# Light convolution and feed-forward: the second product in nine slots a pair, with two banks that swap halves, and the work around it placed anew

## The chip, the cores and the metric

The kernel runs on one core of a Trainium2 chip. The metric is device time of one execution in microseconds (us). The five engines of the core that matter here are TensorE (PE, with its weight loads as PEld), VectorE (DVE), ScalarE (ACT), GpSimd (POOL) and SyncE (SP, which only issues DMAs).

## What is computed

The reference is a depthwise causal convolution of 7 taps (weights by head, through a softmax), then a feed-forward layer with a clipped square between its two products, all in float32:

```python
# x: (8, 4096, 192), weight: (8, 7) -> tokens: 32768 rows of 192
out = np.einsum('hk,bskhg->bshg', softmax(weight), x_unf)   # x_unf: the last 7 rows of each row
# feed-forward, d_ff = 2048
h = x @ w_in
g = np.where(h >= 1, h, np.where(h <= -1, 0.0, (h + 1) ** 2 / 4))
return g @ w_out
```

## The kernel before

**Tiles.** The 32768 tokens are cut into 64 blocks of 512 tokens (`s`). The 2048 hidden channels are cut into 8 pairs (`j`) of two 128-channel chunks (`e`). A step `q` is one pair of one block: 512 steps. Two blocks make a group of 16 steps (`i` = 0 to 15), for which the convolution is worked in three units: "a" (128 channels of the first block), "b" (128 channels of the second) and "r" (the remaining 64 channels of both).

**Precision.** Blocks 0 and 1 (the first 16 steps) use plain float32 matmuls, which cost more passes. The other 62 blocks (496 steps) use float32r operands, each number split in a high part (`hi`, `gh`, first half of `W`) and a low part (`lo`, `gl`), so that a product is high x high + low x high + high x low.

**Two matmuls at a time.** Every matmul contracts 64 rows: one in the upper half of the array's rows (partitions 0 to 63, `TOP`) and its partner in the lower half (`BOT`). The two run side by side and write different PSUM banks. I call such a pair of matmuls a slot.

**A step.** `mm1(q)` makes h for pair q: 18 matmuls, 9 slots, into one of two h buffers of two banks each. `mm2(q - 2)` (`DELAY = 2`) adds the second product of an earlier pair into four accumulator banks: `m0`, `m1` for 128 output channels (one bank for each half of the array), `r0`, `r1` for the other 64 (beside their own low-part product, since 64 channels leave room). That is 20 matmuls, 10 slots: high x high on m in four matmuls a half (the weight's two parts), gl on m in two, gh and gl on r in two each.

**Between the products**, for the later blocks: VectorE clips h to -1..1 (L463), ScalarE squares (L469), VectorE takes the maximum with h (L474); a step later ScalarE casts to the high part (L481) and VectorE subtracts to get the low part (L487). `g`, `gh` and `gl` have three buffers each.

**Accumulators.** After pair 7 of a block, `evac` copies the four banks out on ScalarE (L498, L499), GpSimd adds m0 + m1 and r0 + r1 (L501), ScalarE moves the lower half of r up (L511), GpSimd adds it (L512), VectorE transposes (L524), and SyncE's queue stores.

**The order of the work.** Each engine runs its own instructions in the order in which the code writes them; semaphores do the rest. Tables (`PLAN_A`, `PLAN_B`, `PLAN_R`) say in which of the 16 steps which tap of which unit is done, and when a unit is transposed ("T") or split into high and low parts. A tap is a product on ScalarE (L219, L226 for the first) and an addition on GpSimd (L230). `Chunk.hi` and `Chunk.lo` prepare the weights' parts during the first 16 steps.

## Time and profile before

| | |
|---|---|
| median of three runs | 2256.98 us (2256.78 to 2256.98) |
| the profiled execution: span from first to last instruction | 2255.6 us |
| TensorE busy | 2249.6 us, 100% of the span |
| VectorE busy | 2103.2 us, 93% |
| ScalarE busy | 1697.6 us, 75% |
| GpSimd busy | 1168.4 us, 52% |
| granted TensorE clock | 1.000 |

How to read the profile's rows. A row of a group has the source line, the engine, the operation, its output and inputs by the program's tile names, the shapes and the count; then busy time in us and the mean of one in ns; then the idle time of the engine just before such instructions, and who ended it. A row of a timeline has the start in us, the duration, and the same names; idle time before it stands in brackets with its releaser. A row of a line's own view has the least, median and greatest duration in ns. A row on DMAs has the size and the median time in us from issue to landing. Names ending in q are queues. A matmul's end is modelled, its start is measured.

### The profile page before, as it was taken

The numbers are of one execution on the slowest core, as the hardware profiler recorded it, in microseconds if no ns is written. First come the engines' busy times: TensorE is split into PE (matmuls) and PEld (weight loads), VectorE is DVE, ScalarE is ACT, GpSimd is POOL, SyncE is SP. The second block draws the span as 40 slices with busy tenths as digits, with TensorE's granted clock in tenths as the row PEclk, the third lists the DMA queues.
The fourth block names the chain that finished last, engine by engine and source line by source line (L and its number), as shares of the span: only waits on it lengthen the run. The fifth ranks groups of instructions, "written<-read, shape, count | busy, mean of one in ns | idle before, by whom it ended". The sixth has DMA issues, their size and how long they took to land.

```text
span 2255.6 us, 48202 instructions
## 1 busy us (share of the span) xinstructions
PE 2249.6 (100%) x19645; PEld 1842.2 (82%) x19645; DVE 2103.2 (93%) x1883; ACT 1697.6 (75%) x2153; POOL 1168.4 (52%) x868
## 2 busy tenths in 40 slices
PE   9999999999999999999999999999999999999999
PEld 6988888888888888888888888888888888888887
DVE  8899999999999999999999999999999999999997
ACT  7677877778777787777877777877778777787775
POOL 1446644556445565454654455644556545565441
PEclk9999999999999999999999999999999999999999
DMA  7222222222222212222222222222222222212211
GB/s 158 49 51 48 42 46 47 51 53 39 51 49 46 53 34 51 49 49 51 41 46 47 49 51 51 39 49 46 49 53 39 51 49 46 54 35 50 49 34 24
DMA packets 442125, 110.84 MB, mean 49 GB/s; under 512 B 410288, under 2 KB 417840, under 8 KB 441904
## 3 DMA queue, kind: packets, MB, share of 16 engines
q1 hardware_dynamic: 441744, 107.66, 25.8%
q8 instruction: 155, 2.54, 0.5%
q14 instruction: 66, 0.54, 0.1%
q10 hardware_dynamic: 160, 0.10, 0.0%
HBM read 32.84 MB, written 25.17 MB: 26 GB/s over the span
## 4 chain that ended last, share of the span: by engine, by line
PE 100%; ACT 0%; DVE 0%; issue 0%; DVEq 0%; POOL 0%; POOLq 0%; ACTq 0%
PE h L408 47%; PE accm L452 30%; PE accr L452 20%; PE accr L426 1%; PE accm L426 1%; PE accr L190 0%; PE accm L602 0%; PE accr L408 0%; PE accm L181 0%; PE h L155 0%; PE h L553 0%; PE accr L646 0%; ACT xT L168 0%; ACT xT L165 0%; ACT xT L167 0%
## 5 line engine op out<-in xcount | busy, mean ns | idle before, releaser
L230 POOL TENSOR_TENSOR y<-y,p 128x512 f32<-128x512 f32 x546 | 765.5, 1402 | 730.8 <-DVE g L474 559.5
L487 DVE TENSOR_TENSOR gl<-g,gh 128x1024 fp32r<-128x1024 f32 (+1 forms) x497 | 732.1, 1473 | 27.6 <-ACT gh L481 23.6
L469 ACT ACTIVATE g<-g 128x1024 f32<-128x1024 f32 (+1 forms) x505 | 535.3, 1060 | 242.4 <-DVE g L463 232.9
L463 DVE TENSOR_SCALAR g<-h 128x1024 f32<-128x1024 f32 (+1 forms) x505 | 609.8, 1208 | 97.1 <-PE h L408 88.1
L481 ACT CAST gh<-g 128x1024 fp32r<-128x1024 f32 (+1 forms) x497 | 521.7, 1050 | 237.1 <-DVE g L474 225.6
L408 PE MATMUL h<-hi,w 64*128 64x512 f32 x4032 | 629.8, 389 | 0.0
L474 DVE TENSOR_TENSOR g<-h,g 128x1024 f32<-128x1024 f32 (+1 forms) x505 | 613.4, 1215 | 12.1 <-ACT g L469 4.5
L452 PE MATMUL accm<-gh,w 64*128 64x512 f32 x3966 | 535.0, 388 | 0.0
L408 PEld LDWEIGHTS h<-hi,w 64*128 64x128 f32 x4032 | 382.6, 184 | 81.9
L452 PEld LDWEIGHTS accm<-gh,w 64*128 64x128 f32 x3966 | 372.3, 184 | 81.8 <-issue 0.2
L408 PE MATMUL h<-lo,w 64*128 64x512 f32 x2016 | 399.6, 388 | 0.0
L219 ACT ACTIVATE p<-xT,wk 128x512 f32<-128x512 f32 x562 | 375.1, 710 | 0.0
L452 PE MATMUL accm<-gl,w 64*128 64x512 f32 x1984 | 308.1, 388 | 0.0
L452 PE MATMUL accr<-gl,wr 64*128 64x512 f32 x1984 | 308.0, 388 | 0.0
L452 PE MATMUL accr<-gh,wr 64*128 64x512 f32 x1984 | 308.0, 388 | 0.0
L408 PE MATMUL h<-rh,w 64*128 64x512 f32 x992 | 306.0, 388 | 0.0
L408 PE MATMUL h<-rhi,w 64*128 64x512 f32 x992 | 306.0, 388 | 0.0
L408 PEld LDWEIGHTS h<-lo,w 64*128 64x128 f32 x2016 | 193.3, 184 | 41.5 <-DMA lo<-lo 0.3
L501 POOL TENSOR_TENSOR sum<-t 128x512 f32<-128x512 f32 (+1 forms) x124 | 160.7, 1316 | 126.3 <-ACT t L499 126.3
L452 PEld LDWEIGHTS accm<-gl,w 64*128 64x128 f32 x1984 | 186.4, 184 | 40.9
L452 PEld LDWEIGHTS accr<-gh,wr 64*128 64x128 f32 x1984 | 186.4, 184 | 40.9
L452 PEld LDWEIGHTS accr<-gl,wr 64*128 64x128 f32 x1984 | 186.4, 184 | 40.9
(145 smaller groups left out, 1976.8 us busy)
## 6 DMA issues: line engine op xcount, KB each, us to landing
out_dram<-osb SPq DMA_DIRECT2D x366, 64.0 KB, 2.0
raw<-in_x_dram SPq DMA_DIRECT2D x334, 68.0 KB, 2.4
hi<-hi SPq DMA_DIRECT2D x126, 128.0 KB, 2.3
lo<-lo SPq DMA_DIRECT2D x126, 128.0 KB, 2.3
rhi<-rh SPq DMA_DIRECT2D x62, 128.0 KB, 2.2
rlo<-rl SPq DMA_DIRECT2D x62, 128.0 KB, 2.3
words<-in_moe_w_in_dram SPq DMA_DIRECT2D x16, 192.0 KB, 4.0
words<-in_moe_w_out_dram SPq DMA_DIRECT2D x8, 384.0 KB, 5.0
```

Source lines behind the costliest of these rows:

```text
L219: nc.scalar.mul(p, self.xT[:, SH + k:SH + k + TB], wk[:, self.wsel, k:k + 1])
L230: nc.gpsimd.tensor_add(y, y, self.product(k))
L408: nc.tensor.matmul(h[e], w[HALVES[e], c0:c0 + P], x[e][e], start=(n == 0), stop=(n == len(mms) - 1))
L426: nc.tensor.matmul(accs[s][a, i][:, c0:c0 + D], g[half, e, b * P:(b + 1) * P], w[half, e, :], start=(j == 0 and e == 0 and b % 2 == 0), st ...
L452: nc.tensor.matmul(accs[s][a, i], st, g[HALVES[i], e, :], start=(j == 0 and n == first[a]), stop=(j == NPAIR - 1 and n == last[a]))
L463: nc.vector.tensor_scalar(out=g[:, e, :], in0=hs[q][:, e, :], scalar1=-1.0, scalar2=1.0, op0=ALU.max, op1=ALU.min)
L469: nc.scalar.activation(g[:, e, :], g[:, e, :], AF.Square, bias=0.5, scale=0.5)
L474: nc.vector.tensor_tensor(out=g[:, e, :], in0=h[:, e, :], in1=g[:, e, :], op=ALU.max)
L481: nc.scalar.copy(gh[:, e, :], gs[q][:, e, :])
L487: eng.tensor_sub(gl[:, e, :], g[:, e, :], gh[:, e, :])
L501: nc.gpsimd.tensor_add(y[:, n], t[0][:, n], t[1][:, n])
```

## The change

Seven things change together. `LATE = 3` comes into force after the first two blocks, so `mm2` runs three pairs behind `mm1`.

1. **Nine slots.** w_out's 192 columns are cut into X, Y, Z of 64. The two 128-column weight tiles of a half are arranged so that a pair needs three turns of three slots. In each turn a half has one kind of columns: X and Y, X and Z, or Z and Y, where a stationary tile holds high parts for the one and low parts for the other. The first two slots of a turn are the pair's two chunks with `gh`, the third is with a low part of g: `gl0` or `gl1` for one chunk, or their sum `gt` (a new VectorE addition, L528), with its own weight tile `WL` whose columns come in part by DMA from the high parts of both chunks.
2. **Two banks swap halves.** In the first turn the upper half writes r0 and the lower half r1, in the second m0 and m1, in the third r1 and r0. In odd pairs the turns run the other way round, so that neighbouring pairs begin and end with the same banks. Before the third turn (L474) TensorE waits for a semaphore, `turns`, raised after the second turn's first slot (L481). The source writes this as `drain(fusable=True).then_inc`; in the built program the matmul before it carries the increment and no instruction for the drain is left.
3. **Relu for clip.** ScalarE does relu (L507) and square (L508); VectorE does minimum and maximum in one instruction (L513, `most`). VectorE's clip goes.
4. **Order in a step.** ScalarE: relu and square of q, the accumulators' copies if a block is done, taps, then the cast of q - 1 (before: the cast came first). VectorE: the low part of q - 2 and its sum, transposes and taps, then the maximum of q.
5. **Accumulators.** ScalarE copies the four banks in the order m0, m1, r1, r0 (L552), in step j = 2. The sums are four accumulating DMAs, issued on GpSimd's queue in steps j = 3 and j = 4 (L561); the second two read what the first two wrote. Transposes and stores follow in steps 6 and 7 (before: 2 and 3).
6. **Taps of A on VectorE** (`taps_dve`, L215) from the second group on, and new tables that spread the taps; loads of "a" and "r" are issued two steps earlier.
7. **The weights' parts** are made by other subtractions (L389 to L394) and four small DMAs a chunk; the last block's sum (`evac_last`) is written anew; pools are listed in another order, and the one matmul of 128 rows (`WHOLE`) goes.

The core of the diff:

```diff
+LATE = 3
...
+        def lo(self, rest):
...
+            nc.vector.tensor_sub(w[:, :, 2, x], f[:, :, z], w32[:, :, 1, y])
+            nc.vector.tensor_sub(v[:, 1, x], f[:, 1, x], w32[:, 0, 0, x])
+            nc.vector.tensor_sub(v[:, 2, y], f[:, 0, y], w32[:, 1, 0, y])
+            for to, src in ((v32[:, 0, x], w32[:, 0, 0, x]), (v32[:, 0, y], w32[:, 1, 0, y]),
+                            (v32[:, 1, y], w32[:, 1, 1, y]), (v32[:, 2, x], w32[:, 0, 1, y])):
+                nc.sync.dma_start(out=to, in_=src)
...
+    XY, XZ, ZY = range(3)
+    BANKS = (("r", 0), ("m", 0), ("r", 1)), (("r", 1), ("m", 1), ("r", 0))
+    PARTS_OF = (XZ, XY, ZY), (ZY, XY, XZ)
+    turns = tc.alloc_semaphore("turns")
+    turn = [0]
+
+    def leave(mm):
+        nc.tensor.drain(fusable=True).then_inc(turns, 1)
+        turn[0] += 1
+
+    def enter():
+        nc.tensor.wait_ge(turns, turn[0])
+
     def mm2(q):
...
-        m0, m1, r0, r1, r = ("m", 0, gh), ("m", 1, gh), ("m", 0, gl), ("r", 0, gh), ("r", 0, gl)
-        mms = [(e, m) for ms in ((m0, m1), (r0,), (r1,), (r,)) for e in range(2) for m in ms]
...
+        low = {XY: gt, XZ: gl[:, 1, :], ZY: gl[:, 0, :]}
+        seen = set()
+        for k in range(9):
+            for i, half in enumerate(HALVES):
+                turned = k // 3 if j % 2 == 0 else 2 - k // 3
+                bank, part = BANKS[i][turned], PARTS_OF[i][turned]
+                w, g = ((wg[:, k % 3, part], gh[:, k % 3, :]) if k % 3 < 2
+                        else (wl[:, part], low[part]))
+                if i == 0 and k == 6:
+                    enter()
+                mm = nc.tensor.matmul(accs[s][bank], w[half], g[half],
...
+                if i == 1 and k == 3:
+                    leave(mm)
...
+    def act_both(q):
+        g = gs[q] = act.tile([P, 2, TB], F32, name="g", bufs=3)
+        for e in tiles(q):
+            nc.scalar.activation(g[:, e, :], hs[q][:, e, :], AF.Relu, bias=0.5, scale=0.5)
+            nc.scalar.activation(g[:, e, :], g[:, e, :], AF.Square)
...
+        nc.vector.tensor_add(gt, gl[:, 0, :], gl[:, 1, :])
...
+    def evac_banks(s):
+        acc = accs.pop(s)
+        t = {}
+        for bank in (("m", 0), ("m", 1), ("r", 1), ("r", 0)):
+            t[bank] = ob.tile([P, TB], F32, name="t", bufs=4)
+            nc.scalar.copy(t[bank], acc[bank])
...
+    def evac_add(s, step):
+        t = sums[s] if step == 0 else sums.pop(s)
+        m, r = t["m", 0], t["r", 0]
+        for to, src in (((m, t["m", 1]), (r[BOT], t["r", 1][TOP])) if step == 0 else
+                        ((m[TOP], r[TOP]), (m[BOT], t["r", 1][BOT]))):
+            nc.gpsimd.dma_start(out=to, in_=src, accum_op=ALU.add)
...
-    PLAN_A = {4: ("T", 0), 5: (1, 2), 6: (3, 4), 7: (5, 6), 8: "split"}
+    PLAN_A = {1: ("T",), 2: (0, 1), 3: (2,), 4: (3,), 8: (4,), 9: (5,), 10: (6,), 11: "split"}
...
+            if q < NQ:
+                act_both(q)
+            if done is not None and done % NPAIR == NPAIR - 1:
+                (evac if done < NF32 else evac_banks if done < NQ - 1 else evac_last)(
+                    done // NPAIR)
...
+            if q - 2 in ghs and q - 2 not in gls:
+                act_lo(q - 2)
+            if q < NQ:
+                if s > 2 and j in (3, 4):
+                    evac_add(s - 1, j - 3)
+                m = 6 if s > 2 else 2
+                if m <= j < m + 2:
+                    store(s - 1, "mr"[j - m])
+                conv_slot(i, conv_b, conv_n.get("a"), conv_n.get("r"))
+            if q - 1 in gs:
+                act_hi(q - 1)
+            if q < NQ:
+                act_most(q)
```

How the instructions stand. First TensorE, one second product of an ordinary pair before (`accm` and `accr` are the banks m0, m1 and r0, r1; `w` and `wr` the weight tiles; the lines left out repeat the row above them for the other chunk or part):

```order
L452 MATMUL accm_6749<-gh,w_90 128x512
L452 MATMUL accm_6750<-gh,w_90 128x512
...
L452 MATMUL accm_6749<-gl,w_90 128x512
L452 MATMUL accm_6750<-gl,w_90 128x512
...
L452 MATMUL accr_6751<-gh,wr_98 128x512
L452 MATMUL accr_6752<-gh,wr_98 128x512
...
L452 MATMUL accr_6751<-gl,wr_98 128x512
L452 MATMUL accr_6752<-gl,wr_98 128x512
```

The same place now, in the first pair of a block (`wg` is the tile of `WG`, `words` that of `WL`, `m` is `gt`; what a row waits for stands in brackets):

```order
L475 MATMUL accr_12057<-gh,wg_98 128x512 [waits Activation_49]
L475 MATMUL accr_12058<-gh,wg_98 128x512
...
L475 MATMUL accr_12057<-gl,words 128x512 [waits DVE_49]
L475 MATMUL accr_12058<-gl,words 128x512
L475 MATMUL accm_12055<-gh,wg_98 128x512
L475 MATMUL accm_12056<-gh,wg_98 128x512
...
L475 MATMUL accm_12055<-m,words 128x512 [waits DVE_49]
L475 MATMUL accm_12056<-m,words 128x512
L475 MATMUL accr_12058<-gh,wg_98 128x512 [waits turns]
L475 MATMUL accr_12057<-gh,wg_98 128x512
```

The r banks come first and last, the m banks between; the first slot waits for ScalarE, and the third turn, with the r banks' partners exchanged, for `turns`.

ScalarE around the copies of the accumulators before:

```order
L481 CAST gh<-g 128x1024 [waits DVE_49,PE_49]
L469 ACTIVATE g<-g 128x1024 [waits DVE_49]
L498 COPY t<-accm_9512 128x512 [waits PE_49]
L499 COPY t<-accm_9513 128x512 [waits PE_49]
L498 COPY t<-accr_9514 128x512 [waits PE_49]
L499 COPY t<-accr_9515 128x512 [waits PE_49]
```

And now (DMASW is the semaphore of the accumulating DMAs that last used the copy's tile):

```order
L507 ACTIVATE g<-h 128x1024 [waits DVE_49,PE_49]
L508 ACTIVATE g<-g 128x1024 [waits Activation_49]
L552 COPY t<-accm_5981 128x512 [waits DMASW4_49,PE_49]
L552 COPY t<-accm_5982 128x512 [waits DMASW7_49,DMASW5_49,PE_49]
L552 COPY t<-accr_5984 128x512 [waits DMASW6_49,PE_49]
L552 COPY t<-accr_5983 128x512
L220 ACTIVATE p<-xT,wk 128x512 [waits Pool_49]
L518 CAST gh<-g 128x1024 [waits DVE_49]
```

The cast moved behind the copies, a relu stands ahead of the square, and r0 (`accr_5983`) is copied last.

More of the change, by code (lines that the diff above doesn't have):

```diff
@@ L364, in bits @@
             yield
-        def parts(self, rest):
-            j, k = self.j, n_in[self.j]
-            if rest:
-                yield (WF[j][:, :, 0:P],
-                       *(W[j][:, i, k:].rearrange("p (f d) -> p f d", f=2) for i in range(2)))
-                yield WF[j][:, :, P:], WR[j][:, :, 0], WR[j][:, :, 1]
-            else:
-                yield WI[j], W[j][:, 0, 0:k], W[j][:, 1, 0:k]
-        def hi(self, rest):
-            for w, hi, _ in self.parts(rest):
-                nc.scalar.copy(hi, w)
@@ L379, in lo @@
-        def lo(self, rest):
-            for w, hi, lo in self.parts(rest):
-                nc.vector.tensor_sub(lo, w, hi.bitcast(F32))
+        def hi(self, rest):
+            j = self.j
+            if not rest:
+                nc.scalar.copy(W[j][:, 0], WI[j])
+                return
+            w = WG[j - LAG]
+            nc.scalar.copy(w[:, :, 0], WF[j][:, :, 0:P])
+            nc.scalar.copy(w[:, :, 1, DR:], WF[j][:, :, P:])
+        def lo(self, rest):
+            j = self.j
+            if not rest:
+                nc.vector.tensor_sub(W[j][:, 1], WI[j], W[j][:, 0].bitcast(F32))
+                return
+            n = j - LAG
+            if n % 4 == 0:
+                t = stage.tile([P, 4, 3, P], F32R, name="words", bufs=3)
+                WL.extend(t[:, i] for i in range(4))
+            w, v, f = WG[n], WL[n], WF[j]
+            w32, v32 = w.bitcast(F32), v.bitcast(F32)
+            x, y, z = slice(0, DR), slice(DR, P), slice(P, D)
+            by_block = w.rearrange("p e a c -> p e (a c)").rearrange("p e (k c) -> p e k c", k=2)
+            nc.vector.tensor_sub(by_block[:, :, :, P:],
+                                 f[:, :, 0:P].rearrange("p e (k c) -> p e k c", k=2),
+                                 w32[:, :, 0].rearrange("p e (k c) -> p e k c", k=2))
+            nc.vector.tensor_sub(w[:, :, 2, x], f[:, :, z], w32[:, :, 1, y])
[4 more added lines that the diff above has]
+                nc.sync.dma_start(out=to, in_=src)
@@ L442, in mm2 @@
-        last = {a: max(n for n, (e, m) in enumerate(mms) if m[0] == a) for a in "mr"}
-        for n, (e, (a, part, g)) in enumerate(mms):
-            c0 = k + e * P
-            if q in WHOLE and (e, a, part, n) == (0, "m", 0, 0):
-                nc.tensor.matmul(accs[s][a, 0], w[:, part, c0:c0 + P], g[:, e, :],
-                                 start=False, stop=False)
-                continue
-            for i in range(2):
-                st = (w[HALVES[i], part, c0:c0 + P] if a == "m"
-                      else wr[HALVES[i], e].rearrange("p a d -> p (a d)"))
-                nc.tensor.matmul(accs[s][a, i], st, g[HALVES[i], e, :],
-                                 start=(j == 0 and n == first[a]),
-                                 stop=(j == NPAIR - 1 and n == last[a]))
+        wg, wl = WG[j], WL[j]
@@ L521, in store @@
             return
-        n = P if a == "m" else DR
+        n = slice(0, P) if a == "m" else BOT
         osb = ob.tile([P, TB // SQ, SQ], F32, name="osb")
-        nc.vector.transpose(out=osb[0:n].rearrange("p j b -> p (j b)"), in_=y[0:n])
-        for i in range(n // SQ):
-            c0 = i * SQ + (0 if a == "m" else P)
+        nc.vector.transpose(out=osb[n].rearrange("p j b -> p (j b)"), in_=y[n])
+        for i in range(n.start // SQ, n.stop // SQ):
+            c0 = i * SQ + (0 if a == "m" else DR)
             dst = out[s * TB:(s + 1) * TB, c0:c0 + SQ]
@@ L722, in conv_slot @@
             if ks:
-                u.taps(*ks)
+                (u.taps_dve if u is a and not early else u.taps)(*ks)
     PARTS = {q: [] for q in range(2 * NPAIR + 1)}
@@ L827, in first_step @@
         conv_slot(q, conv_b, conv_n.get("a"), conv_n.get("r"))
-    conv_n = {}
-    for q in range(NQ + DELAY):
+    conv_n, ahead = {}, {}
+    for q in range(NQ + LATE):
         s, j = divmod(q, NPAIR)
         c, i = divmod(q, 2 * NPAIR)
-        done = q - DELAY
         if q < NQ and i == 0 and c > 0:
@@ L836, in lightconv_then_ffn @@
         if q < NQ and i == (0 if c > 0 else 4):
-            conv_n = {}
+            conv_n, ahead = ahead, {}
             if c + 1 < NB:
-                conv_n = {u: Conv(c + 1, u, load_unit(c + 1, u)) for u in "arb"}
+                for u in "arb":
+                    if u not in conv_n:
+                        conv_n[u] = Conv(c + 1, u, load_unit(c + 1, u))
+        if i == 14 and c + 2 < NB:
+            ahead = {u: Conv(c + 2, u, load_unit(c + 2, u)) for u in "ar"}
+        done = q - (DELAY if q < NF32 + DELAY else LATE)
+        if done < 0 or q == NF32 + DELAY:
+            done = None
         if q == NPAIR:
@@ L845, in lightconv_then_ffn @@
             mm1(q)
-        if done >= 0 and q != NPAIR:
+        if done is not None and q != NPAIR:
             (mm2 if done >= NF32 else mm2_first)(done)
```

110 lines of the change are left out of this document (54 added, 56 removed).

## The prediction

> **What bounds the kernel now.** I read the page's busy line and its chain of waits first, then the chain in order of time, then the two engines next in line.
>
> ```profile
> PE 2249.6 (100%) x19645; PEld 1842.2 (82%) x19645; DVE 2103.2 (93%) x1883; ACT 1697.6 (75%) x2153; POOL 1168.4 (52%) x868
> ...
> PE 100%; ACT 0%; DVE 0%; issue 0%; DVEq 0%; POOL 0%; POOLq 0%; ACTq 0%
> ```
>
> The chain that ended last is TensorE alone. No other engine is late anywhere that counts, though VectorE at 93% has little room. The chain in order of time shows the rhythm: one row is the first product of one pair.
>
> ```profile
> 110.09 2.06 PE h L408 x18
> ...
> 288.40 2.06 PE h L408 x18
> ...
> L452 PE MATMUL accm<-gh,w 64*128 64x512 f32 x3966 | 535.0, 388 | 0.0
> L452 PE MATMUL accm<-gl,w 64*128 64x512 f32 x1984 | 308.1, 388 | 0.0
> ```
>
> From 110.09 to 288.40 lie 41 pairs, so a pair takes 178.31 / 41 = 4.349 us. A pair is 18 matmuls of the first product and 20 of the second, and they run two at a time, one in each half of the array: 19 slots, 0.2289 us each. The counts (1984 rows for 4 matmuls a pair) give 496 pairs in this form. The other 16 pairs, in full fp32 at the start, don't change.
>
> **Part 1: nine slots for ten.** The second product goes from 20 matmuls to 18 of the same shape. If TensorE stays without a gap, a pair takes 18 x 0.2289 = 4.120 us, and 496 x 0.2289 = 113.5 us goes. This is also the most the change can gain, since nothing else on TensorE gets shorter. It makes 2256.98 - 113.5 = 2143.5. (The profiled execution has a span of 2255.6 us; the median of the three runs is 1.4 us above it, and I carry that along.) All else is a question of what opens gaps on TensorE.
>
> **Part 2: the wait between the two turns.** In each pair the seventh slot waits for a semaphore which the fourth slot's second matmul raises. In the built program that matmul carries the increment itself; there is no instruction between. Behind the waiting matmul stands everything else of TensorE, so a late release is paid 496 times.
>
> ```profile
> 1207.69 0.39 PE L408 MATMUL h<-rlo,w 64*128 64x512 f32 x1
> 1208.11 1.23 DVE L463 TENSOR_SCALAR g<-h 128x1024 f32<-128x1024 f32 x1 [0.68 <-PE h L408]
> ...
> 7.38 0.58 ACT L168 COPY xT<-h 64x511 f32<-64x511 f32 x1
> ...
> 8.01 0.19 PEld L190 LDWEIGHTS accr<-xT,t 128*128 128x128 f32 x1 [1.57 <-ACT xT L168]
> ...
> L408 PEld LDWEIGHTS h<-hi,w x184: 184/184/186, 1201.3 to 1297.9; 64*128 64x128 f32 x184
> ```
>
> An idle VectorE started 0.42 us after the start of the matmul that released it, and TensorE loaded weights 0.05 us after the ScalarE copy that released it had ended. With the matmul's own 0.39 us, the release reaches TensorE 0.42 to 0.44 us after the fourth slot's start. The seventh slot's weight load starts two slots after the fourth slot (0.458 us), and since a load takes 0.184 of a 0.229 us slot it could start up to 0.045 us later, at 0.503. So the release comes in time, barely. I take nothing; no row has TensorE waiting for itself. A wait can't gain time, so the other end is above: a release 0.15 us later than the rows say stalls 0.09 us a pair, 44 us in all.
>
> **Part 3: ScalarE and the accumulators.** ScalarE takes over the clip: two passes over g where it had one, and still the cast.
>
> ```profile
> L747 ACT ACTIVATE g<-h 128x1024 f32<-128x1024 f32 x7 | 7.1, 1021 | 2.3 <-PE h L408 2.3
> L749 ACT ACTIVATE g<-g 128x1024 f32<-128x1024 f32 x7 | 7.4, 1054 | 0.0
> L481 ACT CAST gh<-g 128x1024 fp32r<-128x1024 f32 (+1 forms) x497 | 521.7, 1050 | 237.1 <-DVE g L474 225.6 <-PE h L408 2.7
> L219 ACT ACTIVATE p<-xT,wk 128x512 f32<-128x512 f32 x562 | 375.1, 710 | 0.0
> L248 ACT CAST hi<-y 128x512 fp32r<-128x512 f32 x63 | 38.1, 605 | 0.9 <-DVE y L214 0.9
> L499 ACT COPY t<-accr 128x512 f32<-128x512 f32 (+1 forms) x63 | 38.2, 607 | 0.0
> ```
>
> In 16 pairs: 16 x (1.02 + 1.05 + 1.05) = 50.0; 14 taps for B and the rest (A's 7 leave) at 0.71 = 9.9; 3 casts at 0.605 = 1.8; 8 copies of accumulators at 0.6 = 4.8. That is 66.5 us of durations against 16 x 4.120 = 65.9 us of TensorE. But neighbours on ScalarE overlap, as its timeline in the step that empties the accumulators shows:
>
> ```profile
> 1209.43 1.06 ACT L469 ACTIVATE g<-g 128x1024 f32<-128x1024 f32 x1 [0.86 <-DVE g L463]
> 1210.40 0.57 ACT L498 COPY t<-accm 128x512 f32<-128x512 f32 x1
> 1210.86 0.59 ACT L499 COPY t<-accm 128x512 f32<-128x512 f32 x1
> 1211.34 0.60 ACT L498 COPY t<-accr 128x512 f32<-128x512 f32 x1
> 1211.82 0.61 ACT L499 COPY t<-accr 128x512 f32<-128x512 f32 x1
> 1212.29 1.08 ACT L481 CAST gh<-g 128x1024 fp32r<-128x1024 f32 x1
> ```
>
> A 1.06 us square is followed after 0.97, a 0.6 us copy after 0.47. About 0.1 us off for some 57 of 73 instructions (a square has to await its relu) leaves 61 us: 92% busy. It keeps up on average, but where work is bunched it is late, and one bunch lies at TensorE's door. Call X the moment when the last pair of a block has issued its nine slots. The first product of the step before began at X - 4.12, its ninth slot at X - 2.29; relu starts 0.42 later, X - 1.87; the square follows at about X - 0.82; 0.97 later, X + 0.15, the four copies start, 0.47 apart, in the order m0, m1, r1, r0. The last one, r0, starts at X + 1.57, ends at X + 2.18, and TensorE sees it at X + 2.23. The next pair's first slot wants r0: its load is due 8 slots after X, at 1.83, at the latest 1.88. TensorE waits 0.36 us, once a block; 61 blocks go this way (x61 at L511 below): 22.0 us. Nothing covers this: the waiting slot is at the head of TensorE's queue. Ends: 0, if only later slots were held; 0.8 if ScalarE comes 0.4 us late to that step, 49 us.
>
> Afterwards ScalarE is 1.35 us behind: the copies (1.9), then a product and a cast. It makes up some 0.5 to 0.9 us a step, and h has two buffers: relu, square and VectorE's maximum must end 8 us after the first product began and end at 5.5. So 2.5 us of slack hide it.
>
> **Part 4: VectorE.** It loses the clip, and gains the sum of the two low parts (512 columns, priced as L263) and seven taps for A.
>
> ```profile
> L487 DVE TENSOR_TENSOR gl<-g,gh 128x1024 fp32r<-128x1024 f32 (+1 forms) x497 | 732.1, 1473 | 27.6 <-ACT gh L481 23.6
> L463 DVE TENSOR_SCALAR g<-h 128x1024 f32<-128x1024 f32 (+1 forms) x505 | 609.8, 1208 | 97.1 <-PE h L408 88.1
> L754 DVE SCALAR_TENSOR_TENSOR g<-g,h 128x1024 f32<-128x1024 f32 x7 | 8.5, 1215 | 0.0
> L263 DVE TENSOR_TENSOR rl<-y,rh 128x512 fp32r<-128x512 f32 x31 | 21.1, 681 | 0.6 <-ACT rh L262 0.6
> L214 DVE SCALAR_TENSOR_TENSOR y<-xT,wk,y 128x512 f32<-128x512 f32 x7 | 5.2, 744 | 0.2
> L524 DVE STREAM_TRANSPOSE osb<-sum 128x512 f32<-128x512 f32 x122 | 85.5, 701 | 3.4
> L147 DVE STREAM_TRANSPOSE xT<-raw 128x544 f32<-128x544 f32 x95 | 69.3, 729 | 0.0
> ```
>
> In 16 pairs: 16 x (1.47 + 0.68 + 1.22) = 53.9; taps 7 x 0.74 = 5.2; transposes 4 x 0.70 + 3 x 0.73 = 5.0; L263 itself 0.7: 64.8 us, below 65.9 even without overlap. Per step: the subtraction awaits the cast of the step before, done 1.8 us into the step, then the sum at 3.1, taps or a transpose, and the maximum at 4.3, when the square is ready. The low parts are wanted a step later still (three pairs of delay for two), with 3 us to spare. Nothing to pay.
>
> **Part 5: the sums by DMA.** GpSimd's additions of accumulators and ScalarE's L511 copy become four accumulating DMAs a block from GpSimd's queue, the second two behind the landing of the first two; GpSimd's additions for taps are queued behind them.
>
> ```profile
> L501 POOL TENSOR_TENSOR sum<-t 128x512 f32<-128x512 f32 (+1 forms) x124 | 160.7, 1316 | 126.3 <-ACT t L499 126.3
> L511 ACT COPY t<-sum 64x512 f32<-64x512 f32 x61 | 37.8, 620 | 1.5
> L230 POOL TENSOR_TENSOR y<-y,p 128x512 f32<-128x512 f32 x546 | 765.5, 1402 | 730.8 <-DVE g L474 559.5
> hi<-hi SPq DMA_DIRECT2D x126, 128.0 KB, 2.3
> words<-in_moe_w_out_dram SPq DMA_DIRECT2D x8, 384.0 KB, 5.0
> ```
>
> Who waits for them is VectorE's output transpose, in step j=6: X + 0.36 + 3 x 4.12 + 3.7 = X + 16.4, and 2.4 us later TensorE. The DMAs can start at X + 2.2, after one GpSimd addition at about X + 3.6. So two rounds of up to 7.6 us are free. The nearest rows give 2.3 to 5.0 us for a landing, without the issue; I take nothing.
>
> **Part 6: ends.** The eight weight chunks' extra subtractions and small DMAs lie in the first 16 pairs, ahead of their use. At the end a third pair of second products replaces other cover, and the last block's sum has an addition more in each half (0.42 us, as L547 below); I put 1.5 us on all of it.
>
> ```profile
> L547 DVE TENSOR_TENSOR t<-accr,t 128x256 f32<-128x256 f32 x2 | 0.8, 418 | 1.2 <-ACT t L546 1.2
> ```
>
> Sum: 2256.98 - 113.5 + 22.0 + 1.5 = 2167.0.
>
> **Rivals.** (a) No wait at the accumulators: 2145. For it: TensorE never waited there in this trace, and 0.36 us is a sum of seven small terms. Against: none of these is in doubt by more than 0.1. (b) Small stalls everywhere: the turn's release 0.03 to 0.09 us late (15 to 44 us), or ScalarE with little of its overlap: 66.5 us of durations and 0.03 of gap behind each relu make 4.19 us a pair, some 12 us over the forecast's average. 2179 to 2211. For it: the margin of 0.04 us in part 2. (c) Slower: the accumulating DMAs. A round of R us ends the chain at X + 3.6 + 2R; past X + 18.8 each us is paid 61 times. The gain of 90 us is used up at 1.48 us a block, R = 8.3; at R = 10 the stall is 4.8 us, 293 us in all, 2460. For it: 256 KB is read and added to another 256 KB, and no such DMA is in the trace. Against: 5.0 us for 384 KB from far away. The Trainium skill, "DMA: Bandwidth & Descriptors", on the anatomy of a DMA from GpSimd, gives 2.0 us + bytes / 436e3, by which I estimate 2.6 us for 256 KB; "SBUF — State Buffer", on its two sides, warns that VectorE can hold up the descriptors such a DMA needs. No run here shows either.
>
> (d) The increment acts as a true drain. Then the fifth slot's load starts 0.44 us after the fourth slot's start in place of 0, and the pair takes 0.44 us more: 218 us, 2385. Against: the increment sits on a matmul. The Trainium skill, "PSUM — Partial Sum Buffer", section "Engine vs sequencer instructions", says that a drain waits until the engine is fully idle; by that rule the source's drain would cost just this, had it been kept apart.
>
> **Numbers.** Forecast 0.54; (a) 0.12; (b) 0.24; (c) 0.07; (d) 0.03. The range goes from (a), less the 3 us by which the ends may be wrong, to (b)'s top with 5 us: 2142 to 2216. A measurement of this kernel tells about 0.2%, 4.5 us, from no change. Faster: the first three and 0.02 of (c): 0.92. Same 0.01. Slower: 0.07.
>
> **What would show it.** Right: pairs 4.12 us apart; once in eight pairs TensorE idle for 0.3 to 0.4 us at the second product's first load, released by ScalarE's copy of r0; no idle at the seventh slot; ScalarE and VectorE both above 90%. Wrong: a gap before each pair's seventh slot (b or d); VectorE's output transpose released by a DMA (c); no gap at the copies (a).

## The result, and the profile after

The kernel after takes 2158.97 us, the median of four runs (2158.73 to 2160.18), against 2256.88 us for the kernel before beside it: a ratio of 0.9567, 95% interval 0.9553 to 0.9581. That is 97.9 us less, and 8 us less than the 2167.0 forecast; the range holds it. The 8 us are what errors of opposite sign left over, as the accounts below show.

The page of the kernel after, its busy line and its chain of waits:

```profile
PE 2138.7 (99%) x18654; PEld 1743.0 (81%) x18654; DVE 1953.5 (91%) x2112; ACT 1974.5 (91%) x2379; POOL 838.4 (39%) x749
...
PE 88%; ACT 5%; DVE 4%; issue 3%; DMA 0%; SPq 0%; DVEq 0%; ACTq 0%
```

TensorE still sets the end, but no longer alone: ScalarE and VectorE appear in the chain, and both are now at 91%. The chain in order of time, from one emptying of the accumulators to behind the next (start, duration, what):

```profile
1001.88 2.04 PE h L423 x18
...
1004.60 0.68 PE accm L475 x6
1005.28 0.68 PE accr L475 x6
1005.96 2.04 PE h L423 x18
...
1026.36 2.04 PE h L423 x18
...
1030.94 1.57 ACT t L552 x3
...
1032.55 0.96 PE accr L475 x6
...
1034.89 2.04 PE h L423 x18
```

Pairs are 4.08 us apart (1001.88 to 1005.96), 18 slots of 0.2267, where the prediction reckoned with 4.12, 18 of 0.2289. Between 1004.60 and 1005.28, where the seventh slot waits for the turns' semaphore, nothing opens. Once in eight pairs the chain leaves TensorE: its next product goes through the four copies, and the pair from 1030.44 (1026.36 + 4.08) to 1034.89 takes 0.37 us more. What TensorE's weight loads waited for (total, times, longest):

```profile
PEld accr L475 <- ACT t L552: 29.1, 59, 0.5
PEld h L423 <- DVE g L805: 9.0, 10, 2.6
```

The first row is the wait of part 3, 0.49 us at the load, in 59 of the 61 blocks. The second was not foreseen: ten waits on VectorE's maximum, four of them with 5.4 us between 95 and 125 us, where the first 16 pairs pass into the new rhythm, and six with 3.5 us between 579 and 1461 us. These six follow places where VectorE itself was held up, such as this one, in its timeline and in GpSimd's:

```profile
576.35 1.82 DVE L215 SCALAR_TENSOR_TENSOR y<-xT,wk,y 128x512 f32<-128x512 f32 x1
```

```profile
576.32 2.99 POOL L231 TENSOR_TENSOR y<-y,p 128x512 f32<-128x512 f32 x2 [0.56 <-ACT p L220]
```

A tap of VectorE that otherwise takes 0.75 us began while GpSimd was adding, and took 1.82. Experiments 3 come back to this. The groups that carried the sum, on the page of the kernel after, with two rows of its DMA issues (count, KB, median us to landing):

```profile
L524 DVE TENSOR_TENSOR gl<-g,gh 128x1024 fp32r<-128x1024 f32 (+1 forms) x497 | 662.2, 1333 | 117.2 <-ACT gh L518 116.9
...
L507 ACT ACTIVATE g<-h 128x1024 f32<-128x1024 f32 (+1 forms) x497 | 509.2, 1025 | 120.8 <-PE h L423 120.8
L805 DVE SCALAR_TENSOR_TENSOR g<-g,h 128x1024 f32<-128x1024 f32 x504 | 607.7, 1206 | 9.7 <-ACT g L508 7.7
...
L528 DVE TENSOR_TENSOR m<-gl 128x512 fp32r<-128x512 f32 x496 | 373.8, 754 | 52.9 <-DVE gl L524 1.8
...
L561 POOL DMA_DIRECT2D t<-t x244 | 206.0, 977 | 21.8 <-ACT t L552 18.7
...
t<-t POOLq DMA_DIRECT2D x183, 128.0 KB, 3.7
...
t<-t POOLq DMA_DIRECT2D x61, 256.0 KB, 3.3
```

L528, the new sum, takes 754 ns in the mean for the 681 of the row that it was priced by (693 where no addition of GpSimd is in its way). The accumulating DMAs land after 3.3 and 3.7 us.

**Accounts.** The starts of the first product's matmuls in the two traces divide the spans. Pair 24 (counted from 0) starts at 122.98 us before and 124.59 after, the last pair, 511, at 2240.88 and 2137.30, and 14.69 and 21.06 us follow. In between lie 487 pairs, 4.3489 and 4.1329 us in the mean, and 61 emptyings.

| term | predicted | measured |
|---|---|---|
| nine slots for ten, 487 pairs by 0.2289 | -111.5 | -111.5 |
| 18 slots a pair 2.2 ns shorter | 0 | -19.5 |
| wait on the copies (61 blocks predicted, 59 measured) | +22.0 | +22.8 |
| waits on VectorE's maximum behind pair 24 | 0 | +2.9 |
| start and end (nine pairs' slots, 2.0, in it) | -0.5 | +8.0 |
| sum | -90.0 | -97.3 |

The wait on the copies costs 0.39 us in each of 59 blocks: 0.34 at the first two slots of the second product (0.459 and 0.339 us in place of 0.227), and 0.04 in some nine slots behind them that take 228 to 235 ns in place of 227. The 2.9 us lie in eight pairs, at the six waits behind 579 us. The spans differ by 97.2.

Theory T: the change gains one slot in each of 496 pairs, pays part of it back at the copies, and everything else in it only keeps ScalarE and VectorE from being late. Rivals: the shorter slot is the new order's own doing (then the change is better than it was reckoned), and the waits have other causes than those named. Twelve runs were made on these questions; each is timed against the kernel before.

### The profile page after: what moved, and what is told of

It is laid out like the page before. It is cut to its first block, busy times and chain, and to the rows that moved or that the text cites. A ratio compares the mean times of both kernels' runs of the same rounds, so it can differ in the third digit from the quotient of the medians.

```text
span 2158.4 us, 46950 instructions
## 1 busy us (share of the span) xinstructions
PE 2138.7 (99%) x18654; PEld 1743.0 (81%) x18654; DVE 1953.5 (91%) x2112; ACT 1974.5 (91%) x2379; POOL 838.4 (39%) x749
## 4 chain that ended last, share of the span: by engine, by line
PE 88%; ACT 5%; DVE 4%; issue 3%; DMA 0%; SPq 0%; DVEq 0%; ACTq 0%
PE h L423 40%; PE accr L475 31%; PE accm L475 15%; ACT t L552 4%; DVE gl L524 1%; DVE g L805 1%; DVE y L215 1%; PE accm L441 0%; PE accr L441 0%; DMA lo<-lo 0%; ACT gh L518 0%; PE accr L191 0%; DMA words<-in_moe_w_out_dram 0%; DVE gl L361 0%; ACT g L507 0%
## 5 line engine op out<-in xcount | busy, mean ns | idle before, releaser
L231 POOL TENSOR_TENSOR y<-y,p 128x512 f32<-128x512 f32 x366 | 526.8, 1439 | 1171.9 <-ACT p L220 1166.0
L524 DVE TENSOR_TENSOR gl<-g,gh 128x1024 fp32r<-128x1024 f32 (+1 forms) x497 | 662.2, 1333 | 117.2 <-ACT gh L518 116.9
L475 PE MATMUL accr<-gh,wg 64*128 64x512 f32 x3968 | 618.8, 390 | 4.2
L507 ACT ACTIVATE g<-h 128x1024 f32<-128x1024 f32 (+1 forms) x497 | 509.2, 1025 | 120.8 <-PE h L423 120.8
L805 DVE SCALAR_TENSOR_TENSOR g<-g,h 128x1024 f32<-128x1024 f32 x504 | 607.7, 1206 | 9.7 <-ACT g L508 7.7
L508 ACT ACTIVATE g<-g 128x1024 f32<-128x1024 f32 (+1 forms) x497 | 527.3, 1061 | 15.8
L475 PEld LDWEIGHTS accr<-gh,wg 64*128 64x128 f32 x3968 | 367.3, 184 | 102.8 <-ACT t L552 29.1
L528 DVE TENSOR_TENSOR m<-gl 128x512 fp32r<-128x512 f32 x496 | 373.8, 754 | 52.9 <-DVE gl L524 1.8
L475 PE MATMUL accr<-gl,words 64*128 64x512 f32 x1984 | 386.8, 387 | 0.4 <-DVE gl L524 0.4
L475 PE MATMUL accm<-gh,wg 64*128 64x512 f32 x1984 | 306.2, 387 | 0.0
L475 PEld LDWEIGHTS accr<-gl,words 64*128 64x128 f32 x1984 | 185.9, 184 | 40.8 <-DVE gl L524 1.3
L561 POOL DMA_DIRECT2D t<-t x244 | 206.0, 977 | 21.8 <-ACT t L552 18.7
L423 PEld LDWEIGHTS h<-rhi,w 64*128 64x128 f32 x992 | 182.5, 184 | 19.5
```

Of the source, the lines that this page charges most:

```text
L231: nc.gpsimd.tensor_add(y, y, self.product(k))
L423: nc.tensor.matmul(h[e], w[HALVES[e], c0:c0 + P], x[e][e], start=(n == 0), stop=(n == len(mms) - 1))
L475: mm = nc.tensor.matmul(accs[s][bank], w[half], g[half], start=(j == 0 and bank not in seen), stop=(j == NPAIR - 1 and k % 3 == 2 and (ban ...
L507: nc.scalar.activation(g[:, e, :], hs[q][:, e, :], AF.Relu, bias=0.5, scale=0.5)
L508: nc.scalar.activation(g[:, e, :], g[:, e, :], AF.Square)
L524: nc.vector.tensor_sub(gl[:, e, :], g[:, e, :], gh[:, e, :])
```

## Experiments 1: where the shorter slot comes from

**e1 and e2.** The kernel before with after's order of pools, and the reverse.

```diff
-    xin = ctx.enter_context(tc.tile_pool(name="xin", bufs=3))
-    xw = ctx.enter_context(tc.tile_pool(name="xw", bufs=2))
     xo = ctx.enter_context(tc.tile_pool(name="xo", bufs=3))
     act = ctx.enter_context(tc.tile_pool(name="act", bufs=2))
     ob = ctx.enter_context(tc.tile_pool(name="ob", bufs=2))
+    xw = ctx.enter_context(tc.tile_pool(name="xw", bufs=2))
+    xin = ctx.enter_context(tc.tile_pool(name="xin", bufs=3))
```

> The kernel before, with one edit: the pools xw and xin are declared after xo, act and ob, as in the changed kernel, so these tiles lie elsewhere in SBUF. In the changed kernel a slot takes 0.2267 us, before 0.2289 us, which the prediction had not foreseen. Theory A (where the tiles lie sets the cadence): slots of 0.2267 us here too, 9424 slots less 2.2 ns each, about 21 us, so 2236. Theory B (the cadence comes from the weights' tiles or from the order of matmuls, not from the pools): slots stay at 0.2289 us and the time at 2257.

> The changed kernel with the pools in the order of before (xin and xw ahead of xo). Theory A (place sets the cadence): slots of 0.2289 us, 8928 slots with 2.2 ns more each, about 20 us, so 2179. Theory B: no change, 2159 and 0.2267 us.

Measured: e1 2298.69 us, ratio 1.0186 (1.0171 to 1.0201), 42 us longer; e2 2196.09, 0.9732 (0.9717 to 0.9746). Neither theory of e1 holds as it was put: the order of pools does matter, with not one instruction changed, but it makes the kernel before slower. What it moves is the place of the tiles in SBUF. In the built programs the moving operands' tiles (`hi`, `lo`, `rh`, `rl`, `gh`, `gl`) start at byte 192 modulo 256 before, 0 after, 64 in e1, 128 in e2. It looked as if that place decided.

**e5.** The kernel before with these tiles, and all that are allocated behind `whose`, 64 bytes further on:

```diff
-    whose = const.tile([P, 2 * P + 3 * K + 3], F32, name="whose")[:, 0:2 * P]
+    whose = const.tile([P, 2 * P + 3 * K + 3 + 16], F32, name="whose")[:, 0:2 * P]
```

> The kernel before with 16 floats of padding more on one early tile, so that every tile allocated behind it moves by 64 bytes: the moving operands of both products then start at 0 modulo 256 (192 in the kernel before), the stationary ones stay at 128 (in the kernel after they lie at 0). Nothing else differs. Theory P (the start address of the moving operand modulo 256 sets the slot's length: 228.9 ns at 192, 226.7 at 0, 233.3 at 64, 231.0 at 128, as the kernel before, after, e1 and e2 gave): 226.7 ns a slot, 496 pairs of 19 slots by 2.2 ns are 21 us less, about 2236 us. Rival Q (the stationary operand's place is what counts, or both together): the slot stays at 228.9 or takes another length, and the time stays at 2257 or rises. Rival R (the cadence of after comes with its order of slots, not with a place): 2257.

Measured: 2289.87, 1.0145 (1.013 to 1.0161). Theory P falls: at 0 modulo 256 the slot is longer, not shorter. The weight tiles lie at 128 modulo 256 in the kernel before and in e1 and e5, at 0 in the kernel after and in e2. That left the distance between the two operands, and gave e9 and e10.

**e9** takes 16 floats off the padding in place of adding them (`3 * K + 3 - 16`); **e10** adds 16 floats to the same tile of the kernel after (`const.tile([P, 2 * P + 16], ...)[:, 0:2 * P]`).

> The kernel before with 16 floats less of padding on one early tile: the moving operands now start at 128 modulo 256, as the stationary ones do; nothing else differs. Theory P (the moving operand's own place decides) has fallen with e5; as it was put it would give 231.0 ns a slot, 2277 us. Theory D (what decides is the distance of the moving operand's start from the stationary one's, modulo 256: 226.7 ns at 0 (after), 228.9 at 64 (before), 231.5 to 232.4 at 128 (e2, e5), 233.3 at 192 (e1)): distance 0, 226.7 ns a slot, 2236 us. Rival S (both places count in some other way, such as their sum): any other length, 229 to 233 ns, 2257 to 2299 us.

> The kernel after with 16 floats of padding on one early tile: moving operands at 64 modulo 256, the stationary ones at 0, but those of the low parts' slots at 64 too. Theory D: distance 64 in 15 of a pair's 18 slots, 0 in 3; 228.5 ns a slot in the mean, 18 by 1.8 ns by 488 pairs are 16 us more, 2175 us, less a few us of the wait on the copies, which come due later: 2170 to 2176. Rival S: another length, up to 233 ns: 2176 to 2215. Rival (the place plays no part in the new order of slots): 2159.

Measured: e9 2235.77, 0.9906 (0.9891 to 0.9921); e10 2174.19, 0.9634 (0.9617 to 0.965). Both come within 1 us of what theory D gave. Two pairs, ten pairs apart, in the chains of e1 and e9:

```profile
1000.86 2.10 PE h L408 x18
...
1045.20 2.10 PE h L408 x18
```

```profile
1000.78 2.04 PE h L408 x18
...
1043.85 2.04 PE h L408 x18
```

The 44.34 and 43.07 us between them, divided by 190 slots, are 0.2334 and 0.2267 us. Sorted by the distance of the two operands' starts, with the same instructions in the same order in all variants of a kernel:

| kernel | moving | weights | distance mod 256 | slot, ns |
|---|---|---|---|---|
| after, e9 | 0, 128 | 0, 128 | 0 | 226.7, 226.7 |
| before, e10 (15 of 18 slots) | 192, 64 | 128, 0 | 64 | 228.9, 228.9 |
| e2 (17 of 18 slots), e5 | 128, 0 | 0, 128 | 128 | 232.0, 232.4 |
| e1 | 64 | 128 | 192 | 233.3 |

The moving operand's place alone doesn't decide (0 gives 226.7 or 232.4 ns, 128 gives 232.0 or 226.7), and the weights' place alone doesn't. That it is the distance is not shown: the weights start at 0 or 128 in all these slots, and for these two the sum of both places, which rival S names, sorts the kernels in the same way. In e10 three slots of a pair have both operands at 64. By the distance they should take 226.7 ns, by the sum 232; their medians are 229, 226 and 229, and those of the first product's slots with `lo`, at distance 64, are 229 as well. So the rule holds for a kernel's mean slot, and not slot by slot.

So the 19.5 us are the change's, but not the nine slots': they come with where its tiles happen to lie, and the kernel before gets 21 us from one number in a padding.

## Experiments 2: the terms of the sum

**e7: ten slots again.**

```diff
-        for k in range(9):
+        for k in (0, 1, 2, 3, 4, 5, 6, 7, 7, 8):
...
-                                            and (bank[0] == "m" or k == 8)))
+                                            and (bank[0] == "m" or k >= 8)))
```

> The kernel after with the eighth slot of each second product issued twice, so ten slots for nine; the two parts of the product that belong to that slot are counted twice in the output. Theory (a slot is worth 0.2267 us wherever TensorE has no gap, and the evacuation's wait shrinks by the slot that a pair grows): 496 by 0.2267 is 112.4 us more, less up to 0.23 us of wait in 61 blocks (the copies are then due a slot later, and ScalarE has 8 slots more in a block) which is 5 to 14 us: 2257 to 2266 us. Rival (a slot is worth 0.2289 us, as in the kernel before, and what makes after faster than its sum lies elsewhere): 113.5 and no less wait: 2272. Rival (in after TensorE is no longer what bounds, so a slot is in part free): below 2245.

Measured: 2254.4, 0.9988 (0.9979 to 0.9998); this kernel counts the products of the repeated slot twice, so its output is not the reference's. A slot more costs 95.4 us: 112.4, less 17.0. Nearly all of that comes back in TensorE's waits, above all at the copies, where the wait shrinks to 16.4 us in 61 blocks at the loads:

```profile
PEld accr L475 <- ACT t L552: 16.4, 61, 0.3
```

The pair's mean is 4.3258 us, 19 by 0.2267 and 0.019 for the waits, in place of 0.053. This is the theory, 3 us past its end. With the slot back nothing is left of the gain, although each slot is still 2.2 ns shorter than in the kernel before.

**e4: the increment one slot later.**

```diff
-                if i == 1 and k == 3:
+                if i == 1 and k == 4:
```

> The changed kernel with the semaphore of the turns raised one slot later (by the fifth slot in place of the fourth). Theory of the prediction (the release comes 0.42 to 0.44 us after its matmul's start, with a margin of some 0.04 us): the seventh slot's load starts at 0.227 + 0.43 = 0.66 us in place of 0.50 at the latest, 0.16 us a pair, 79 us in all: 2238. Rival (TensorE sees its own matmul's end sooner than other engines do, so the margin is over a slot): 2159.

Measured: 2230.89, 0.9887 (0.987 to 0.9903), 72 us more. The wait that was absent is there. The one on the copies is gone, and in 59 pairs TensorE waits for VectorE's low part instead:

```profile
PEld accr L475 <- PE accm L475: 112.6, 433, 0.3
PEld accm L475 <- DVE gl L524: 31.2, 59, 0.5
```

The medians of a pair's 18 slots add up to 4.25 us, 0.17 more. A slot is 0.23, so in the kernel after the release came some 0.06 us before it was needed, or 0.11 if the 0.05 are left out that slower slots behind the wait make of the 0.17. Part 2's margin (0.04, at the latest 0.08) has the right size, and it is thin.

**e6: a true drain.**

```diff
-        nc.tensor.drain(fusable=True).then_inc(turns, 1)
+        nc.tensor.drain(fusable=False).then_inc(turns, 1)
```

> The kernel after with the increment of the semaphore on a drain of its own that may not be joined with the matmul before it. Rival (d) of the prediction, taken literally: the fifth slot's load starts only when TensorE is empty, 0.44 us after the fourth slot's start in place of 0.23 behind it, some 0.42 to 0.44 us a pair for 496 pairs, 208 to 218 us more: 2367 to 2377 us, with the gap between the fourth and the fifth slot of each pair. Rival: a drain in the instruction stream costs its issue and the emptying of two slots only, 0.05 to 0.25 us a pair: 2184 to 2283. Nothing: 2159.

Measured: 2323.82, 1.0297 (1.0279 to 1.0314): 164.9 us more, slower than the kernel before. The fourth and fifth slots at one drain, in TensorE's timeline, the fifth slot's weight load, and the row in the view of waits:

```profile
1001.92 0.98 PE L475 MATMUL accm<-gh,wg 64*128 64x512 f32 x4
```

```profile
1002.39 0.19 PEld L475 LDWEIGHTS accm<-gh,wg 64*128 64x128 f32 x2 [0.50 <-issue]
```

```profile
PEld accm L475 <- issue: 249.2, 496, 0.5
```

From the fourth slot to the fifth it is 0.484 us in place of 0.227, to the sixth 0.331; the pair's medians add up to 4.47, 0.39 more than 18 slots. Of the 193 us this makes, some 26 come back, since the copies now have time and no wait of TensorE names them any more. Rival (d) had the place right and 0.44 for 0.39. The rule that the prediction quoted from the Trainium skill, "PSUM — Partial Sum Buffer", section "Engine vs sequencer instructions" (a drain waits until the engine is idle), agrees with the trace: the fourth slot's matmuls begin at 1001.92 and take 0.39 us, and the fifth slot's load begins at 1002.39, just behind their end. The change is a gain only because the increment rides on the matmul.

**e12: tokens A back on ScalarE and GpSimd.**

```diff
-                (u.taps_dve if u is a and not early else u.taps)(*ks)
+                u.taps(*ks)
```

> The kernel after with the taps of tokens A undone: products on ScalarE and additions on GpSimd, as in the kernel before, where the change has them on VectorE. Theory (that part was needed: ScalarE, 91% busy, has no room): 7 products of 0.61 us more in 16 pairs, 4.3 us, on the 61 that it has, against 65.4 us of TensorE at 226.7 ns a slot, so ScalarE full, and each wait for its relu now paid: 4.10 to 4.25 us a pair in place of 4.133, 2165 to 2220 us, with waits on the copies above 0.5 us and on the maximum. Rival (hidden, since ScalarE keeps up on the average and VectorE gains 5.2 us of room): 2155 to 2163. Rival (slower by far: 31 more additions in GpSimd's queue hold up VectorE): above 2220.

Measured: 2268.07, 1.005 (1.0035 to 1.0065). Without this part the nine slots gain nothing at all. The rival "slower by far" is the nearest, and both its engines show. TensorE's waits in e12:

```profile
PEld h L423 <- DVE g L805: 84.2, 151, 1.0
PEld accm L475 <- DVE m L528: 42.4, 63, 1.2
```

The subtraction's group, from the view by lines:

```profile
L524 DVE TENSOR_TENSOR gl<-g,gh 128x1024 fp32r<-128x1024 f32 (+1 forms) x497 | 789.3, 1588 | 215.0 <-ACT gh L518 212.1
```

VectorE waits 212 us for ScalarE's cast (in the kernel after 117), and its subtraction takes 1.59 us in the mean (1.33), while GpSimd has 180 more additions (546 for 366). VectorE has lost 154 us of taps, yet is busy for 1970.0 us against 1953.5. The next section shows that this second thing is a thing of its own. The other parts around the slot (relu for clip, the order in a step, the sums by DMA, the third pair of delay) were not undone one by one; that they only serve the slot is not shown.

## Experiments 3: the wait on the copies, and what stands behind it

**e3: the banks that are wanted first are copied first.**

```diff
-        for bank in (("m", 0), ("m", 1), ("r", 1), ("r", 0)):
+        for bank in (("r", 0), ("r", 1), ("m", 0), ("m", 1)):
```

> The changed kernel with the accumulators copied in the order r0, r1, m0, m1 in place of m0, m1, r1, r0. Theory of the prediction (the next pair's first slot waits for the last copy, r0, once a block): the wait of 0.34 us and the slower slots behind it go, 0.42 us a block, 61 blocks, 26 us: 2133, and TensorE's waits on L552 vanish. Rival (ScalarE is late there anyway, and the wait moves to the m banks or to the next step's h): 2150 to 2159.

Measured: 2163.13, 0.9586 (0.9571 to 0.96): 4 us slower than the kernel after. The wait on the copies is gone, and another one has its place:

```profile
PEld h L423 <- DVE g L805: 45.3, 92, 2.6
```

The chain of e3 from the copies on shows how it gets there:

```profile
1031.54 1.58 ACT t L552 x3
1033.12 0.61 ACT p L220
1033.73 0.94 ACT gh L518
1034.70 1.56 DVE gl L524
...
1056.58 1.81 DVE y L215
...
1060.87 1.53 issue
...
1063.14 1.14 DVE g L805
1064.32 2.34 PE h L423 x18
```

The copies make ScalarE's cast late, the cast makes VectorE's subtraction late, and VectorE, with next to no room, carries that from one maximum to the next for seven pairs, until TensorE finds no free buffer for h. But the chain holds a second thing: a tap of 1.81 us for 0.74, and behind it a gap of 1.53 us in which the sum of the low parts took 1.71 for 0.69. Both began while GpSimd was adding. In e3 this happens to 24 taps and 59 sums, in the kernel after to 4 and 32. Of the 1.43 us that TensorE waits for the maximum between 1038 and 1065 us, in two blocks, 0.12 stand ahead of any tap or sum so held up, 0.27 behind a sum that is held up in the kernel after too, and 1.05 behind these two. So most of the wait comes from where the lateness puts VectorE, into additions of GpSimd that the kernel after mostly misses. How the ring would do without them was not run. In the kernel after, part 3's "2.5 us of slack hide it" holds for most blocks, where TensorE has just waited 0.39 us itself.

**e8: less work behind the copies.** The order of e3, and the table without ScalarE's products in the steps behind the copies (its third line, `PLAN_R`, changes too); the very end is edited as well (each engine copies one bank).

```diff
-    PLAN_B = {0: (0, 1), 1: (2,), 2: (3,), 3: (4,), 4: (5, 6), 5: "split"}
-    PLAN_A = {1: ("T",), 2: (0, 1), 3: (2,), 4: (3,), 8: (4,), 9: (5,), 10: (6,), 11: "split"}
+    PLAN_B = {0: (0, 1), 1: (2, 3), 3: (4,), 4: (5, 6), 5: "split"}
+    PLAN_A = {1: ("T", 0), 4: (1, 2), 5: (3,), 8: (4,), 9: (5, 6), 11: "split"}
```

> The kernel after with the accumulators copied in the order r0, r1, m0, m1 (as e3), and the table of the convolution's work changed so that the steps just behind the copies (steps 2, 3, 10 and 11 of sixteen) hold no products for ScalarE and no taps for VectorE beyond their last; at the very end ScalarE copies whole pieces of one bank and VectorE of the other. No work is added or left out. Theory (e3 failed only because ScalarE, a step behind after the copies, hands the late cast on to VectorE's subtraction, maximum and so to h's buffer, and free steps there let it catch up): no wait on the copies and none on the maximum: 2159 less 25.8 for the wait and slower slots in 61 blocks, less 2 at the end: 2131, between 2128 and 2140. Rival (the bunch only moves: taps pushed into other steps make those late): 2150 to 2165. Rival (the wait on h is not from that ring but from the copies themselves, 1.9 us on a ScalarE that is 92% busy): as e3, 2163.

Measured: 2245.93, 0.9952 (0.9937 to 0.9966), 87 us slower than the kernel after, and far outside all that was expected. The same instructions make VectorE busy for 2082.5 us in place of 1953.5, and TensorE waits for its maximum:

```profile
PEld h L423 <- DVE g L805: 130.9, 121, 1.5
```

VectorE's timeline and GpSimd's at one place:

```profile
1026.57 0.69 DVE L528 TENSOR_TENSOR m<-gl 128x512 fp32r<-128x512 f32 x1
1027.18 1.79 DVE L215 SCALAR_TENSOR_TENSOR y<-xT,wk,y 128x512 f32<-128x512 f32 x1
...
1031.34 1.60 DVE L528 TENSOR_TENSOR m<-gl 128x512 fp32r<-128x512 f32 x1
```

```profile
1026.75 1.66 POOL L231 TENSOR_TENSOR y<-y,p 128x512 f32<-128x512 f32 x1 [1.37 <-ACT p L220]
1030.74 1.65 POOL L231 TENSOR_TENSOR y<-y,p 128x512 f32<-128x512 f32 x1 [2.32 <-ACT p L220]
```

Both long VectorE rows began while a GpSimd addition ran. Counted over e8's trace from 110 us on: of the taps (L215), 58 began within a GpSimd addition and took 1.73 us in the mean, 120 did not and took 0.74; of the sums (L528), 61 took 1.60 and 432 took 0.69. In the kernel after only 4 taps and 32 sums are caught. The maximum (L805), which reads h from PSUM, takes 1.21 and 1.20. The subtraction (L524) takes 1.58 for 1.21, and the first tap of a unit (L213), one tile with the tap's weight, 1.33 where it is caught and 0.48 in the kernel after, where it never is. So a tap or a sum of VectorE waits about a microsecond if it starts within an addition of GpSimd, and the table had put taps where the additions are. This is the rule of the Trainium skill, "SBUF — State Buffer", section "Who interferes with whom": VectorE's second SBUF input comes through a port shared with GpSimd, and whoever is late waits for the whole instruction. The trace agrees for L215, L528 and L524, which have two inputs in SBUF, and for L805, which has one.

**e11: one copy on VectorE.** The order of e3, the table as in the kernel after, and bank m1 copied by VectorE (what `last_copy` holds) ahead of its maximum, with the very end as in e8; the part that copies the banks:

```diff
-        for bank in (("m", 0), ("m", 1), ("r", 1), ("r", 0)):
+        for bank in (("r", 0), ("r", 1), ("m", 0), ("m", 1)):
             t[bank] = ob.tile([P, TB], F32, name="t", bufs=4)
-            nc.scalar.copy(t[bank], acc[bank])
+            if bank == ("m", 1):
+                last_copy.append((t[bank], acc[bank]))
+            else:
+                nc.scalar.copy(t[bank], acc[bank])
```

> The kernel after with the accumulators copied in the order r0, r1, m0 on ScalarE, and m1 on VectorE ahead of that step's maximum; the table of the convolution's work stays as it is; at the very end ScalarE copies whole pieces of one bank and VectorE of the other. No work is added or left out. Theory (the wait on the copies and the wait on the maximum in e3 are one ring: ScalarE's cast comes late by as much as ScalarE spends on copies, and 0.47 us less there is enough; VectorE has a hole of 1.1 us in the step behind): both waits gone, 25.8 us less and 1 less at the end: 2132, between 2128 and 2140. Rival (the maximum of that very step, 0.6 us later, becomes the late one): 0.2 to 0.4 us a block stay, 2145 to 2160. Rival (GpSimd's additions get in the way of more of VectorE's instructions, as in e8, where 58 taps that began within such an addition took 1.73 us in place of 0.75): 2160 to 2200.

Measured: 2132.22, 0.9448 (0.9434 to 0.9462): 26.8 us below the kernel after, as the theory said to within 1 us. No row of TensorE's waits names the copies any more, the maximum has 7 waits left, and pairs stay 4.08 us apart across an emptying (two pairs in 8.16). The chain of e11, its waits, and the copy's group:

```profile
1018.29 2.04 PE h L423 x18
...
1026.45 2.04 PE h L423 x18
```

```profile
PEld h L423 <- DVE g L813: 6.8, 7, 2.7
```

```profile
L515 DVE COPY t<-accm 128x512 f32<-128x512 f32 x61 | 41.7, 683 | 0.1
```

A copy of 0.68 us that reads PSUM, on the engine that then had a hole of 1.1 us, takes 0.47 us off the engine at which the ring begins, and both waits go. Only 2 taps and 31 sums are caught by GpSimd here, so e11 does not tell the ring's own lateness from what it pushes into the additions; it shows that both begin at the copies.

## Why the prediction was right, and where not

**Part 1, nine slots: right in kind, the slot mis-sized.** One slot in each pair goes (e7). The step that failed is the assumption "of the same shape", so 0.2289 us: the changed order of pools and paddings moved the operands to a distance of 0 modulo 256, and each of the 18 slots that stay became 2.2 ns shorter, 19.5 us in all (distance or sum, as said above). "This is also the most the change can gain, since nothing else on TensorE gets shorter" was wrong. e10, with most slots at the old length, takes 2174.19: this is about what the change gives without that accident, 7 us above the forecast.

**Part 2, the turns' wait: right.** No wait in the trace, and a margin that e4 puts at 0.06 to 0.11 us.

**Part 3, ScalarE: right.** The wait was to be 0.36 us a block in the order m0, m1, r1, r0; it is 0.39 in 59 blocks, slower slots behind it included: 22.8 us for 22.0. ScalarE's timeline there, and the start of the next first product in TensorE's, which is X (1030.44 above is the end of the slot before, from which the chain counts):

```profile
1029.50 1.06 ACT L508 ACTIVATE g<-g 128x1024 f32<-128x1024 f32 x1
1030.47 1.06 ACT L552 COPY t<-accm 128x512 f32<-128x512 f32 x2
1031.41 1.09 ACT L552 COPY t<-accr 128x512 f32<-128x512 f32 x2
```

```profile
1030.28 0.62 PE L423 MATMUL h<-hi,w 64*128 64x512 f32 x4
```

The copies start at X + 0.19 and the last one ends at X + 2.22 (1032.50), against 0.15 and 2.18 in the prediction; the slots being shorter, TensorE came for it 0.02 earlier too. The second step that failed stands behind it, "So 2.5 us of slack hide it". It counted the distance of one maximum from its own deadline, as if VectorE were free to move, and left out that VectorE hands its lateness on and that, once late, it meets GpSimd's additions. It cost little here, because the first wait covers most of it; e3 shows the price, e11 the way out.

**Part 4, VectorE: right**, 91%, and TensorE waits on it at the change of rhythm (5.4 us) and six times more (3.5 us at the loads). The sum missed one thing that e3, e8 and e12 bring out, and that stands behind these six: VectorE's durations depend on when GpSimd adds. It worked the other way too, as the subtraction, priced at 1.47 us, took 1.33. **Part 5, the accumulating DMAs: right.** They were to have 7.6 us a round; two issues of 0.98 and a landing of 3.3 to 3.7 fit easily, and (c) is out. The estimate worked out from the Trainium skill, "DMA: Bandwidth & Descriptors", section "Anatomy of one DMA — SWDGE (gpsimd) path", was 2.6 us for 256 KB; the row of this trace says 3.3.

**Part 6, the ends: mis-sized.** 1.5 us was put on them, and they cost 10.0 (8.0, and the 2.0 of nine pairs' slots that they swallowed). From the chain of the kernel after in its last ten microseconds:

```profile
2148.31 0.43 DVE t L594
...
2148.76 0.37 ACT t L595
```

VectorE and ScalarE take turns at pieces of the same banks, each behind the other; with whole banks for each engine e11 ends 2.9 us sooner (18.15 us behind the last pair's start for 21.06). One more pair of second products alone, 2.04 us, was in the prediction's words and hardly in its number.

**The rivals.** (a), no wait at the copies, gives what e11 measures, once that wait is really taken away: its 2145, with 19.5 us less for the shorter slots and, by e11's trace, some 5.5 more for the ends and the waits left on the maximum, is 2131, and e11 takes 2132.22. (b) didn't come; e4 shows that its first half, a late release, stood 0.06 to 0.11 us away. (d) is e6.

## What to carry to other kernels

Price a slot by the trace of before, but look whether the change moves the operands' tiles: the same matmuls ran at 226.7 to 233.3 ns here, by where moving operand and weights start modulo 256, and one number in a padding is worth 1% of this kernel. A wait that goes uncovers the next one in the same ring, so follow the ring round (copies, cast, subtraction, maximum, buffer) before counting the gain, and take work off the engine where it begins. When work is moved between steps on VectorE, look which GpSimd instruction runs at that time: the durations of the trace of before hold only for the neighbours that they were measured with.

## What the runs showed that was not expected

- A kernel's mean slot goes with the distance of the two operands' starts in SBUF (or their sum): 226.7, 228.9, 232.0 to 232.4 and 233.3 ns at 0, 64, 128 and 192 modulo 256. Distances other than multiples of 64 were not tried, single slots don't follow the rule in e10, and why it is so stays open.
- Behind a stall of TensorE some nine slots are longer: 228 to 235 ns in place of 227 after the copies' wait, 2.5 us in 59 blocks. Behind the two slots that e6's drain holds up, the next four take 233, 232, 232 and 230.
- VectorE's taps and sums, with two SBUF inputs, take 0.9 to 1.0 us longer when they start within a GpSimd addition (0.69 to 1.60, 0.74 to 1.73); the maximum, with an input in PSUM, doesn't (1.21 and 1.20). In e8 this costs more than the whole wait that its table was to remove.
